# Attention in front of two expert layers: scores in two head orientations, heads alternating in the products with V

## The chip, the cores and the metric

The kernel runs on one core of a Trainium2 chip. The metric is the device time of one execution in microseconds (us). Five engines work side by side and wait for one another through semaphores: PE (TensorE, the matrix multiplier, an array of 128 rows by 128 columns), DVE (VectorE), ACT (ScalarE), POOL (GpSimd) and SP (SyncE, which issues most DMA transfers here). PE reads its operands from on-chip memory and writes into PSUM, which has 8 banks; DVE and ACT read PSUM, POOL can't.

## The reference

Causal attention over 4 sequences of 576 positions with 8 heads of 64, then two layers on the 2304 tokens. Cut to what matters:

```
scores = q @ k.T / 8                                  # per batch and head
cum    = cumsum(max(s, 0))
scores = where(causal, -1e9, scores + min(-(cum_i - cum_j), 0))
attn   = softmax(scores)                              # sum + 1e-9
x      = (attn @ v), heads side by side               # 2304 x 512
h      = x @ w_in;  g = elu(h);  x = g @ w_out        # first layer, 512 -> 2048 -> 512
P      = exp(x @ w_gate), 8 rounds of row and column normalisation
out    = sum over 8 experts of P[:, e] * (relu(x @ w1[e]) @ w2[e])
```

## The kernel before, in words

**Attention.** A job is one pair of heads of one batch: 20 jobs in five chunks. Batch 0 is split in chunk A (queries 0 to 255, 4 jobs) and chunk B (queries 256 to 575, 4 jobs); batches 1 to 3 are F chunks (all queries, 4 jobs each). A job's queries go in items of 64 (an index m from 0 to 8); item m looks at 64(m+1) keys, because of the causal mask. In an item the two heads lie on the two halves of the 128 partitions. There are 144 items.

What an item goes through, with its lines:

- `r_step` (lines 235 to 249): POOL writes a tile R with the bias from cumulated s (line 244, over the item's keys) and adds the causal mask to the last 64 keys (line 247). The tile is one of NR = 6 buffers. The rows of cum that it reads come by DMA (line 222), two per job.
- `qk_piece` (lines 251 to 293): PE forms the scores S, one product per head (line 262): 64 rows by 64 columns of the array each, head 0 in the upper left quarter, head 1 in the lower right one. They are of type fp32, and the trace shows each such product as two matmul instructions. The item of 576 keys takes two PSUM tiles of 288. The pool `ps_s` has two PSUM banks. Then DVE adds S to R and finds the extreme (line 268), ACT takes the exponential with its sum (line 276), DVE the reciprocal (lines 280 and 281), and POOL normalises (line 284).
- `t_piece` (lines 301 to 344): PE transposes R in blocks of 128 keys (line 307). An item with an odd number of 64-key blocks has half a block left, for which 64 columns of the array are used (line 313). ACT copies whole blocks into the tiles aA and aB (lines 319 to 326), DVE the half ones (line 337).
- `pv_piece` (lines 351 to 382): the products X with V, in two halves of the queries (`half` 0: 256 queries, lines 365 and 366; `half` 1: 320 queries, lines 369 to 371). Each uses 128 rows by 64 columns of the array, head 0 in the left columns and head 1 in the right; the last block of line 371 has 64 rows. A call does one head, and a half is two calls one after the other, which the order of the work may separate. The result goes to the x of the first layer through ACT and DVE (`split`, lines 375 to 379).

**Order.** `pieces` (lines 386 to 400) lists score items, transposes four items later (LAG = 4), and products with V. The first layer is a list of groups of 12 matmuls (lines 592 and 624, type fp32r, 128 by 128, with n = 256, 288 or 320 columns). In the main loop the pieces of a chunk are spread over the groups ahead of the first group that needs the chunk (lines 1116 to 1152); `_Flow` is a planner with assumed costs and due times, and it decides when the steps after a matmul are put in the program. The framework that turns the program into queues may then issue work that is ready ahead of work that isn't. The first layer's weights are unpacked by DVE and ACT (`w_decode`, lines 519 to 558) as their turn comes.

**The rest.** After the last attention chunk come the remaining groups of the first layer, a gate, and the second layer (experts), which is matmuls of lines 938 and 1007.

Of the kernel before, what the change touches and what calls it, by code (L numbers as in the profile page):

```python
# [92 lines left out]
def kernel(  # L93
# [16 lines left out]
    NR, LAG, NQK, NCB, NSCAN, NA_T, NH = 6, 4, 2, 2, 1, 1, 5  # L110
# [45 lines left out]

    chunks = CHUNKS
# [3 lines left out]
    spans = {"A": range(0, HALF_A // 64), "B": range(HALF_A // 64, S // 64), "F": range(S // 64)}  # L161
# [3 lines left out]
    for j, (k, b, p, part) in enumerate(jobs):  # L165
# [3 lines left out]
    LAST = S // 64 - 1  # L169
# [3 lines left out]
    cum_m = cst.tile([P, S // 64, B * NPAIR], F32, tag="cum_m", name="cum_m")  # L173
# [7 lines left out]
            att.tile([64, 2, 64], F32, tag=f"a4{i}", name=f"a4{i}"),  # L181
# [29 lines left out]
    def cum_advance():  # L211
        while state["cum"] < NJ:
# [5 lines left out]
            t = att.tile([P, S], F32, tag="cum", name=f"cum{j}", bufs=NCB)  # L218
# [15 lines left out]

    def r_step(i):

        if i >= NI:
            return
        j, m = items[i]
        k, b, p, part = jobs[j]  # L240
        t = att.tile([P, S], F32, tag="R", name=f"R{i}", bufs=NR)
        Rt[i] = t
        n = 64 * (m + 1)
        nc.gpsimd.tensor_scalar(out=t[:, 0:n], in0=ct[j][:, 0:n], scalar1=8.0,  # L244
                                scalar2=cum_m[:, m, b * NPAIR + p : b * NPAIR + p + 1],
# [5 lines left out]
    def qk_piece(i):  # L251
        j, m = items[i]
        sm = att.tile([P, 8], F32, tag="sm", name=f"sm{i}", bufs=6)
        keys = 64 * (m + 1)
        parts = [(0, 288), (288, 288)] if m == LAST else [(0, keys)]
        pss = []
        for c0, n in parts:
            ps = ps_s.tile([P, 512], F32, tag="S", name=f"S{i}_{c0}")
            pss.append(ps)
            for z in range(2):  # L260
                r = slice(64 * z, 64 * z + 64)
                nc.tensor.matmul(ps[r, 0:n], QK[j][r, 0, 64 * m : 64 * m + 64], QK[j][r, 1, c0 : c0 + n],  # L262
                                 start=True, stop=True)
        R = Rt[i]

        def ttr():
            for z, (c0, n) in enumerate(parts):
# [3 lines left out]
            if len(parts) == 2:  # L271
                nc.vector.tensor_tensor(out=sm[:, 2:3], in0=sm[:, 0:1], in1=sm[:, 1:2], op=ALU.min)
# [22 lines left out]
    def qk_cost(i):  # L295
        return 4 * 64 * (items[i][1] + 1) / 2400.0
# [912 lines left out]
```

## Time and profile before

| what | value |
|---|---|
| median of 3 runs | 2264.2 us (2262.67 to 2267.24) |
| the profiled execution | 2263.91 us |
| its span in the trace | 2262.1 us |
| mean granted clock of TensorE | 0.992 of full speed |
| instructions in the trace | 33423 |
| PE busy | 2228.7 us, 99% of the span |
| DVE, ACT, POOL busy | 57%, 42%, 36% of the span |

The profiled execution lies 0.3 us below the median, and 1.8 us of it are outside the span. Times in the trace are counted from the start of the span. A busy PE isn't PE at its full rate: consecutive matmuls overlap, so what an operation costs is read from start to start.

### The profile page before, as it was taken

The numbers are of one execution on the slowest core, as the hardware profiler recorded it, in microseconds if no ns is written. First come the engines' busy times: TensorE is split into PE (matmuls) and PEld (weight loads), VectorE is DVE, ScalarE is ACT, GpSimd is POOL, SyncE is SP. The second block draws the span as 40 slices with busy tenths as digits, with TensorE's granted clock in tenths as the row PEclk, the third lists the DMA queues.
The fourth block names the chain that finished last, engine by engine and source line by source line (L and its number), as shares of the span: only waits on it lengthen the run. The fifth ranks groups of instructions, "written<-read, shape, count | busy, mean of one in ns | idle before, by whom it ended". The sixth has DMA issues, their size and how long they took to land.

```text
span 2262.1 us, 33423 instructions
## 1 busy us (share of the span) xinstructions
PE 2228.7 (99%) x12236; PEld 1920.5 (85%) x12236; DVE 1292.5 (57%) x2891; ACT 943.0 (42%) x2133; POOL 815.9 (36%) x1045
## 2 busy tenths in 40 slices
PE   7999999999999999999999999999999999999999
PEld 3467888887889888888989988889898888998988
DVE  7677687434665765555555455555555555555554
ACT  5554444333442454334343443443443533434332
POOL 7664222232320433343333333333333333333330
PEclk9999999999999899999999999999999999999999
DMA  6443344133274432122223322212214212121121
GB/s 224 137 153 117 125 163 144 54 98 109 85 252 146 139 111 66 56 75 68 72 68 135 120 75 65 75 56 66 75 66 168 98 57 75 66 75 66 58 73 38
DMA packets 99668, 224.36 MB, mean 99 GB/s; under 512 B 8304, under 2 KB 24176, under 8 KB 99504
## 3 DMA queue, kind: packets, MB, share of 16 engines
q1 hardware_dynamic: 94896, 205.45, 27.7%
q10 hardware_dynamic: 4608, 16.78, 1.9%
q8 instruction: 96, 1.57, 0.3%
q14 instruction: 68, 0.56, 0.1%
HBM read 184.90 MB, written 37.30 MB: 98 GB/s over the span
## 4 chain that ended last, share of the span: by engine, by line
PE 94%; DVE 3%; POOL 1%; DMA 1%; issue 1%; ACT 0%; SPq 0%; POOLq 0%; DVEq 0%; ACTq 0%
PE b L1007 35%; PE A L938 17%; PE C L938 9%; PE m L592 9%; PE n L624 8%; PE B L938 4%; PE S L262 4%; PE X L369 3%; PE T L307 2%; PE gate L704 1%; PE X L365 1%; PE X L370 0%; DMA xc_d<-xs 0%; DMA xr<-x_d 0%; PE X L371 0%
## 5 line engine op out<-in xcount | busy, mean ns | idle before, releaser
L1007 PE MATMUL b<-w,h 128*128 128x512 f32 x3456 | 846.1, 393 | 0.0
L1007 PEld LDWEIGHTS b<-w,h 128*128 128x128 f32 x3456 | 645.3, 188 | 125.9
L821 POOL TENSOR_TENSOR w1c<-S,w1c 128x512 fp32r<-128x512 f32 x192 | 264.3, 1400 | 871.1 <-ACT w1c L820 871.1
L938 PE MATMUL A<-xc,w1c 128*128 128x384 f32 x2304 | 449.3, 335 | 0.0
L1021 DVE SCALAR_TENSOR_TENSOR acc<-b,P_t,acc 128x512 f32<-128x512 f32 x264 | 197.4, 748 | 424.8 <-PE b L1007 424.8
L938 PEld LDWEIGHTS A<-xc,w1c 128*128 128x128 f32 x2304 | 405.9, 188 | 8.5
L951 ACT ACTIVATE h<-pre_P 128x384 fp32r<-128x384 f32 x288 | 151.3, 525 | 437.1 <-DVE pre_P L964 437.1
L592 PEld LDWEIGHTS m<-xT,w 128*128 128x128 f32 x1536 | 213.9, 193 | 27.3 <-issue 9.4
L592 PE MATMUL m<-xT,w 128*128 128x288 f32 (+2 forms) x1536 | 234.4, 306 | 2.2 <-DVE r L604 1.1
L938 PE MATMUL C<-xc,w1c 128*128 128x384 f32 x1152 | 233.4, 336 | 0.0
L624 PE MATMUL n<-h,w 128*128 128x288 f32 (+2 forms) x1536 | 226.9, 300 | 3.1 <-DVE r L604 1.6
L624 PEld LDWEIGHTS n<-h,w 128*128 128x128 f32 x1536 | 207.4, 188 | 25.9 <-issue 16.6
L938 PEld LDWEIGHTS C<-xc,w1c 128*128 128x128 f32 x1152 | 205.3, 189 | 8.1
L821 DVE TENSOR_TENSOR w<-sw,w 128x512 fp32r<-128x512 f32 x192 | 154.1, 824 | 61.5 <-ACT w L820 61.5
L244 POOL TENSOR_SCALAR R<-cum,cum_m 128x64 f32<-128x64 f32 (+8 forms) x144 | 91.5, 635 | 223.0 <-PE T L313 176.3
L954 DVE SCALAR_TENSOR_TENSOR h<-pre_P,h 128x384 fp32r<-128x384 f32 x288 | 160.9, 559 | 12.2 <-ACT h L951 0.5
L284 POOL TENSOR_SCALAR R<-R,sm 128x64 f32<-128x64 f32 (+8 forms) x144 | 95.9, 668 | 103.0 <-DVE sm L281 78.5
L951 ACT ACTIVATE h<-A 128x384 fp32r<-128x384 f32 x96 | 47.2, 492 | 193.7 <-PE A L938 193.7
L262 PE MATMUL S<-QK 64*64 64x288 f32 (+8 forms) x640 | 119.3, 440 | 8.6 <-DMA QK<-in_qk_dram 4.6
L820 ACT CAST w<-sw 128x512 fp32r<-128x512 f32 x192 | 109.4, 618 | 22.1 <-DMA w<-w_sc 8.7
L972 ACT COPY pre_P<-A 128x384 f32<-128x384 f32 x192 | 92.3, 481 | 60.5 <-PE A L938 60.5
L938 PE MATMUL B<-xc,w1c 128*128 128x384 f32 x576 | 116.4, 336 | 0.0
(163 smaller groups left out, 2367.4 us busy)
## 6 DMA issues: line engine op xcount, KB each, us to landing
sw<-in_w_dram SPq DMA_DIRECT2D x192, 512.0 KB, 3.3
w<-w_sc SPq DMA_DIRECT2D x56, 512.0 KB, 3.5
w_sc<-w ACTq DMA_DIRECT2D x32, 512.0 KB, 3.0
xc_d<-xs SPq DMA_DIRECT2D x28, 384.0 KB, 3.7
xc<-xc_d SPq DMA_DIRECT2D x14, 768.0 KB, 6.4
QK<-in_qk_dram SPq DMA_DIRECT2D x16, 576.0 KB, 4.6
st<-in_wi_dram SPq DMA_DIRECT2D x16, 512.0 KB, 3.7
st<-in_wo_dram SPq DMA_DIRECT2D x16, 512.0 KB, 4.1
```

The costliest lines, as they stand in the source:

```text
L262: nc.tensor.matmul(ps[r, 0:n], QK[j][r, 0, 64 * m : 64 * m + 64], QK[j][r, 1, c0 : c0 + n], start=True, stop=True)
L284: nc.gpsimd.tensor_scalar(out=R[:, 0:keys], in0=R[:, 0:keys], scalar1=sm[:, 5:6], scalar2=1.0, op0=ALU.mult, op1=ALU.mult)
L592: nc.tensor.matmul(ps[:, 0:n], t[:, a, d * P : (d + 1) * P], x[:, z, d, c0 : c0 + n], start=(d == 0 and o == 0), stop=(d == 3 and o == 2))
L624: nc.tensor.matmul(ps[:, 0:n], t[:, a, f * P : (f + 1) * P], h[:, z, c0 : c0 + n], start=(f == 0 and o == 0), stop=(f == 3 and o == 2))
L820: nc.scalar.copy(hi, x)
L821: eng.tensor_tensor(out=lo, in0=x, in1=f32(hi), op=ALU.subtract)
L938: nc.tensor.matmul(ps, t[:, a, wi_, kt * P : (kt + 1) * P], x[:, z, kt], start=(first and kt == 0 and o == 0), stop=(kt == 1 and o == 2), ...
L951: nc.scalar.activation(h[:, 0], src, AF.Relu)
L954: nc.vector.scalar_tensor_tensor(out=h[:, 1], in0=src, scalar=0.0, in1=f32(h)[:, 0], op0=ALU.max, op1=ALU.subtract)
L972: nc.scalar.copy(new(name), ps)
L1007: nc.tensor.matmul(ps, h[:, z, c0 : c0 + P], t[:, a, :], start=(f == 0 and o == 0), stop=(f == 3 and o == 2))
L1021: nc.vector.scalar_tensor_tensor(out=a, in0=ps, scalar=q, in1=a, op0=ALU.mult, op1=ALU.add)
```

## The change

Items are gathered in sets whose scores are issued together. In the B and F chunks the items 0, 1, 3, 6 and 7 have the two heads swapped on the partitions (`swapped`): head 0's scores go to partitions 64 to 127 and head 1's to 0 to 63, which are the two quarters of the array that the other items don't use. A set has a PSUM bank for each orientation. An F job has three sets, a B job three, an A job two (no item swapped). The rows of cum and the per-item scalars exist in both orders, so a B or F job loads two more rows of cum. The bias tiles of items 0 to 4 of an F job share one large buffer (`Rs`, one buffer), NR goes from 6 to 5 with 640 columns, and the bias is written over whole 128-key blocks. The last block of a transpose is 128 wide. Where an item is swapped, its copies after the transpose are made per head. The products with V alternate the heads at each step, in one call, all in the shape 128 by 64 (`a4` has 128 partitions, of which the lower half is zero). Transposes come one set later (two sets in chunk A) instead of four items later, and a product with V that is due is put right in front of the next set's scores.

```diff
-    NR, LAG, NQK, NCB, NSCAN, NA_T, NH = 6, 4, 2, 2, 1, 1, 5
+    NR, NQK, NCB, NSCAN, NA_T, NH = 5, 2, 2, 1, 1, 5
...
+    TAIL = 512
+    SWAP = (0, 1, 3, 6, 7)
+
+    SETS = {"A": [[0, 1], [2, 3]], "B": [[4], [5, 7, (LAST, TAIL)], [LAST, 6]],
+            "F": [[0, 1, 2, 3, 4], [5, 7, (LAST, TAIL)], [LAST, 6]]}
...
-            for z in range(2):
-                src = s if j < NSCAN else cum_d
-                nc.sync.dma_start(t[64 * z : 64 * z + 64, 0:keys],
-                                  src[row + z : row + z + 1, 0:keys].partition_broadcast(64))
+            for w in range(1 if part == "A" else 2):
+                n = TAIL if w else keys
+                for z in range(2):
+                    h = row + (z ^ w)
+                    nc.sync.dma_start(t[64 * z : 64 * z + 64, w, 0:n],
+                                      src[h : h + 1, 0:n].partition_broadcast(64))
...
-        nc.gpsimd.tensor_scalar(out=t[:, 0:n], in0=ct[j][:, 0:n], scalar1=8.0,
+        w = (n + 127) // 128 * 128
+        z = swapped(i)
+        nc.gpsimd.tensor_scalar(out=t[:, 0:w], in0=ct[j].rearrange("p w k -> p (w k)")[:, S * z : S * z + w], scalar1=8.0,
...
+    def qk_set(n):
+        banks, streams, cols = {}, {}, {}
+        for i, c0, keys in sets[n]:
+            z = swapped(i)
+            if z not in banks or cols[z] + keys > 512:
+                banks[z] = ps_s.tile([P, 512], F32, tag="S", name=f"S{i}_{c0}")
+                cols[z] = 0
...
+        while any(streams.values()):
+            z = min((z for z in streams if streams[z]), key=lambda z: done[z])
...
+            for h in range(2):
+                r = slice(64 * h, 64 * h + 64)
+                o = slice(64 * (h ^ z), 64 * (h ^ z) + 64)
+                nc.tensor.matmul(ps[o, at : at + keys], QK[j][r, 0, 64 * m : 64 * m + 64],
+                                 QK[j][r, 1, c0 : c0 + keys], start=True, stop=True)
...
+        def by_head(x, out, eng):
+            if z:
+                for h in range(2):
+                    eng(out[:, h], x[:, 1 - h])
+            else:
+                eng(out, x)
...
-            for c in range(3):
-                nc.tensor.matmul(x[r, 0:320], vj[:, h, c], aB[:, h, c, :], start=(c == 0), stop=False)
-            nc.tensor.matmul(x[r, 128:320], vj[:, h, 3], aB[:, h, 3, 128:320], start=False, stop=False)
-            nc.tensor.matmul(x[r, 256:320], vj[0:64, h, 4], a4[:, h, :], start=False, stop=True)
...
+            steps = [(c, aB[:, :, c, :], 0, 320) for c in range(3)]
+            steps += [(3, aB[:, :, 3, 128:320], 128, 320), (4, a4, 256, 320)]
+        for n_, (c, a, x0, x1) in enumerate(steps):
+            for h in range(2):
+                nc.tensor.matmul(x[64 * h : 64 * h + 64, x0:x1], vj[:, h, c], a[:, h], start=(n_ == 0),
+                                 stop=(n_ == len(steps) - 1))
...
-    for i in range(NI + LAG + 2):
-        if i < NI:
-            pieces.append((jobs[items[i][0]][0], qk_cost(i), "qk", i))
+    for n in range(len(sets) + 4):
+        due = []
+        while pend and pend[0][0] <= n:
+            _, j, half = pend.pop(0)
+            due.append((jobs[j][0], pv_cost(j, half), "pv", (j, half)))
+        if n < len(sets):
+            due.append((set_chunk[n], set_cost(n), "qk", n))
+        if due:
+            bundles.append(due)
+        while emitted < len(sets) and emitted + (2 if set_chunk[emitted] == 0 else 1) <= n:
```

## Rows read from the trace of the kernel before

**Rows 1.** The page, parts 1 and 4: engines, and the chain that ended last.
```profile
PE 2228.7 (99%) x12236; PEld 1920.5 (85%) x12236; DVE 1292.5 (57%) x2891; ACT 943.0 (42%) x2133; POOL 815.9 (36%) x1045
...
PE 94%; DVE 3%; POOL 1%; DMA 1%; issue 1%; ACT 0%; SPq 0%; POOLq 0%; DVEq 0%; ACTq 0%
```

**Rows 2.** Windows: length, PE, PEld, DVE, ACT, POOL busy, granted clock, DMA share, GB/s.
```profile
0.00:39.00 39.00, 25.63 (x122) 13.03 (x122) 26.98 (x104) 17.05 (x56) 25.51 (x61) 0.96 0.64 213
39.00:107.00 68.00, 65.10 (x360) 34.17 (x359) 47.36 (x181) 37.98 (x102) 46.52 (x78) 1.00 0.50 166
107.00:205.00 98.00, 98.00 (x590) 61.12 (x590) 75.55 (x277) 54.86 (x156) 66.38 (x108) 1.00 0.44 147
205.00:425.00 220.00, 220.00 (x1503) 182.68 (x1502) 153.29 (x461) 94.73 (x246) 61.21 (x108) 1.00 0.36 123
425.00:590.00 165.00, 164.98 (x1110) 133.30 (x1109) 79.80 (x283) 64.25 (x175) 48.83 (x95) 0.97 0.30 94
```

**Rows 3.** Timeline of PE, 299 to 309 us: start, length, instruction, count.
```profile
299.62 0.65 PE L262 MATMUL S<-QK 64*64 64x256 f32 x4
300.20 1.70 PE L592 MATMUL m<-xT,w 128*128 128x256 f32 x12
...
303.80 0.76 PE L262 MATMUL S<-QK 64*64 64x320 f32 x4
304.49 2.02 PE L592 MATMUL m<-xT,w 128*128 128x320 f32 x12
306.44 1.83 PE L369 MATMUL X<-aB,V 128*64 128x320 f32 x6
...
308.78 4.58 PE L624 MATMUL n<-h,w 128*128 128x256 f32 x36
```

**Rows 4.** Timeline of PE, 317 to 342 us.
```profile
317.17 3.68 PE L592 MATMUL m<-xT,w 128*128 128x320 f32 x24
320.69 0.27 PE L313 MATMUL T<-ident,R 128*64 128x128 f32 x1
...
327.93 0.27 PE L307 MATMUL T<-ident,R 128*128 128x128 f32 x1
328.04 0.27 PE L313 MATMUL T<-ident,R 128*64 128x128 f32 x1
328.07 2.01 PE L624 MATMUL n<-h,w 128*128 128x320 f32 x12
330.00 1.08 PE L262 MATMUL S<-QK 64*64 64x512 f32 x4
331.01 3.79 PE L624 MATMUL n<-h,w 128*128 128x320 f32 x24
...
341.19 0.65 PE L365 MATMUL X<-aA,V 128*64 128x256 f32 x2
...
341.99 1.85 PE L592 MATMUL m<-xT,w 128*128 128x288 f32 x12
```

**Rows 5.** Timeline of PE, 39 to 41 us: head 0's L366 beside head 1's L365.
```profile
39.97 0.32 PE L366 MATMUL X<-aA,V 128*64 128x128 f32 x1
39.98 0.43 PE L365 MATMUL X<-aA,V 128*64 128x256 f32 x1
40.13 0.27 PE L366 MATMUL X<-aA,V 128*64 128x128 f32 x1
40.25 0.38 PE L365 MATMUL X<-aA,V 128*64 128x256 f32 x1
```

**Rows 6.** Groups by line and shape: operation, count, busy us, mean ns, idle before.
```profile
L268 DVE CUSTOM_DVE_ANT_0 R<-S,R 128x512 f32<-128x512 f32 x16 | 11.0, 689 | 3.7 <-PE S L262 1.9 <-POOL R L247 1.5
...
L326 ACT COPY aB<-T 128x256 f32<-128x256 f32 x16 | 5.9, 370 | 12.7 <-PE T L313 12.5
```

**Rows 7.** DMA issues: transfers of cum, count, KB each, us to landing.
```profile
cum<-cum_d SPq DMA_DIRECT2D x32, 144.0 KB, 3.2
```

**Rows 8.** Waits of PE's weight loads: engine, line waited for, us, times, longest.
```profile
PEld T L307 <- POOL R L284: 12.3, 11, 2.5
```

More of the change, by code (lines that the diff above doesn't have):

```diff
@@ L252, in qk_piece, with softmax @@
+    def softmax(i, c0, n, ps, base):
         j, m = items[i]
-        sm = att.tile([P, 8], F32, tag="sm", name=f"sm{i}", bufs=6)
         keys = 64 * (m + 1)
[L255 to L263, printed above, removed]
@@ L285, in norm, with set_cost @@
                                     op0=ALU.mult, op1=ALU.mult)
-        c = qk_cost(i)
         d = keys / 950.0
-        flow.after(c + 0.05, ttr)
-        flow.after(c + 0.25 + d, ex)
-        flow.after(c + 0.6 + 2 * d, rec)
-        flow.after(c + 0.8 + 2 * d, norm)
-        return c + 1.2 + 3.2 * d
-    def qk_cost(i):
-        return 4 * 64 * (items[i][1] + 1) / 2400.0
+        flow.after(base, ttr)
+        if last:
+            flow.after(base + 0.2 + d, ex)
+            flow.after(base + 0.55 + 2 * d, rec)
+            flow.after(base + 0.75 + 2 * d, norm)
+            ready["t", i] = flow.now + base + 1.15 + 3.2 * d
+        return base + 0.1 + n / 950.0
+    def set_cost(n):
+        t = [0, 0]
+        for i, c0, keys in sets[n]:
+            t[swapped(i)] += keys
+        return 4 * max(t) / 2400.0
     def t_cost(i):
-        return (items[i][1] // 2 + 1) * 0.06
+        return (items[i][1] // 2 + 1) * 0.11
     def t_piece(i):
@@ L383, in pv_piece @@
             flow.after(pv_cost(j, half) + 0.1, lambda: v_load(j + 2))
-    pieces = []
+    sets, set_r, set_t = [], [], []
+    set_chunk = []
+    for j, (k, b, p, part) in enumerate(jobs):
+        at = {m: job_items[j][0] + x for x, m in enumerate(spans[part])}
+        seen_r = set()
+        for x in SETS[part]:
+            parts = [(m, 0) if isinstance(m, int) else m for m in x]
+            sets.append([(at[m], c0, 64 * (m + 1) - c0 if c0 else min(TAIL, 64 * (m + 1))) for m, c0 in parts])
+            set_r.append([at[m] for m, _ in parts if m not in seen_r])
+            seen_r |= {m for m, _ in parts}
+            set_t.append([at[m] for m, c0 in parts if not c0])
+            set_chunk.append(k)
@@ L401 @@
[L401 to L402 removed]
+            due.append((jobs[j][0], pv_cost(j, half), "pv", (j, half)))
[4 more added lines that the diff above has]
+        while emitted < len(sets) and emitted + (2 if set_chunk[emitted] == 0 else 1) <= n:
+            for t in set_t[emitted]:
+                j, m = items[t]
+                for x in [x for x in pend if x[1] != j and x[2] == (m > 3)]:
+                    pend.remove(x)
+                    bundles.append([(jobs[x[1]][0], pv_cost(*x[1:]), "pv", x[1:])])
+                bundles.append([(jobs[j][0], t_cost(t), "t", t)])
+                if m == 3 or t == job_items[j][1] - 1:
+                    pend.append((n + 1, j, 0 if m == 3 else 1))
+            emitted += 1
@@ L403 @@
+    assert not pend
+    chunk_cost = [sum(c for x in bundles for kk, c, _, _ in x if kk == k) for k in range(NCHUNK)]
+    chunk_last = [max(i for i, x in enumerate(bundles) if any(y[0] == k for y in x)) for k in range(NCHUNK)]
     ready = {}
```

180 lines of the change are left out of this document (102 added, 78 removed).

## The prediction

> **What bounds the kernel now.** I read the page first: PE is busy in 99% of the span and holds 94% of the chain that ended last [rows 1]. So a microsecond of PE time that goes is a microsecond of span, as long as nothing else takes over. Then I cut the attention's part of the span into stages with the view by windows [rows 2]. Up to 39 us PE is busy in 25.6 of 39 us: chunk A waits for its own chain. From 39 to 107 us (mostly chunk B) and from 107 to 205 us (the first F chunk) PE is full, but DVE is at 70% and 77% and POOL at 68% in both. From 205 to 425 us and from 425 to 590 us, with four F jobs each, PE is full, DVE at 70% and 48%, POOL under 30%. The reader is to see that PE binds everywhere after 39 us, with little room behind it before 205 us and much after. Behind 590 us there is no attention, and nothing there changes.
>
> Last I read the timeline of PE from start to start, where it never idles [rows 3, 4].
>
> **Scores.** 256 keys take 0.58 us (299.62 to 300.20) and 512 keys 1.01 us (330.00 to 331.01) [rows 3, 4]: 1.68 ns a key and 0.15 us besides. The neighbours pay too: two groups of 12 matmuls of 320 columns take 3.52 us undisturbed (317.17 to 320.69), 1.76 each [rows 4], but the one between scores and X takes 1.95 (304.49 to 306.44) [rows 3]. That is 0.19 more, so a visit of PE to a small shape costs 0.34 us beside its columns. An F job before: 2880 keys, 4.84 us, and nine visits, 3.06, together 7.90. After, if the two orientations overlap: three sets, each as long as its longer stream of 512 keys, 0.86 + 0.34 = 1.20, together 3.60. It saves 4.3 us a job. If they don't overlap, only six visits go, 2.0 us a job; that is the other bound. I take the first: in the rows the two heads of one item already share the array, since a key takes four matmul columns (two heads, two instructions each), and at the pace of X below, 0.3 us for 320 columns, these would take 3.8 ns one after the other and not 1.68.
>
> **Products with V.** One head of half 1 takes 2.34 us (306.44 to 308.78) and, with 0.19 at the neighbours, 2.53; one head of half 0 0.80 (341.19 to 341.99) and 0.99 [rows 3, 4]. Its six matmuls of 320 columns fill 1.83 us of that [rows 3], 0.3 each: they go one after the other. Alternating, both heads should take what one takes: 3.5 us less per F job. The bound below is no gain. I take the gain because the trace holds one place where the queue had head 0's L366 and head 1's L365 side by side: they start 0.01 us apart, at 39.97 and 39.98, and L365's second matmul follows 0.27 us after its first although L366 runs beside it [rows 5]. Both use all 128 rows, each its own 64 columns.
>
> The Trainium skill (TensorE: Matmul & The Clock Gate, section The mechanism) says that weight loads overlap running matmuls only where the row group differs, and that matmuls start and end strictly in program order. By that, alternating heads on the same rows would gain nothing here and the sum would be some 36 us smaller; the starts above speak against it.
>
> **Transposes.** A whole block takes 0.11 us (327.93 to 328.04). A half one takes 0.03 and makes the next group longer: 1.93 against 1.76 (328.07 to 330.00), of which the score visit behind it has about half [rows 4]. So a half block costs 0.03 to 0.20, likeliest 0.11; over 80 of them the change gains or loses up to 7 us. I take nothing.
>
> **Other engines.** Split copies: five more on ACT and two more on DVE per F job, each at most the 0.37 us of a copy of 256 columns, the nearest row [rows 6]: below 2 us on ACT and 0.8 on DVE. POOL writes 320 more columns of 2880 per F job in one of its three steps, below 11% of its time; both hide behind PE after 205 us and add to the load before. Two more loads of cum for each of 16 jobs land in 3.2 us [rows 7] and are issued a job ahead; uncovered, the first B job would pay that once. SP issues them between weights, none of which PE waited for long. What is late next is DVE: a set needs all its additions of S before the next set gets its two banks, up to 0.69 us each [rows 6].
>
> **The sum, by stage.** An F job loses 4.3 + 3.5 = 7.8 us of PE. A B job: five visits and 2240 keys, 5.46, become three sets (320, 512, 512 keys), 3.28; with 2.5 from X it loses 4.7. An A job loses two visits and 0.99, 1.7.
> - 0 to 39 us: PE isn't the bound; between 0 and 7, I take 2.
> - 39 to 107 us: PE would shrink by 19, to 49, with DVE's 47.4 and POOL's 46.5 inside it. No row shows DVE over 77%; at that it needs 61.5 us, a saving of 6. Between 6 and 19, I take 9.
> - 107 to 205 us: PE falls by 31 to 67, below DVE's 75.6. At 77% DVE saves nothing, at 100% 22. I take 13, which is 85 us with DVE at 89%: its rows here are many small steps of separate items, so some of its idle time can be filled.
> - 205 to 590 us: 62, with DVE at 81% of the first 189 us; I take 60.
>
> Together 84 us. The profiled execution took 2263.9 us, 0.3 below the median, and becomes 2180 us.
>
> **The rivals.**
> 1. PE stays the bound throughout and the early stages keep their PE savings: 7 + 19 + 31 + 62 = 119 us, 2145 us. For it: POOL and DVE aren't full now. Against it: both would have to be at 95% or more.
> 2. DVE takes over. It has the additions of S, the copies, the unpacking of weights and the first layer's results, and none of that shrinks. Held at 77%, the stages give 2, 6, 0, 21 and 31 us, 60 in all, 2204 us. For it: [rows 2]. Against it: 77% is what DVE was asked for, not what it can do. The Trainium skill (TensorEngine Tiling (Array Packing), section PSUM Bottleneck) warns that tiling speeds up the array and not the emptying of PSUM, which may then be the bottleneck.
> 3. The two orientations don't overlap, because they read the same rows of the array, or because the framework issues them apart: 2.3 us less in each of eight jobs and some 5 in the early stages, 2203 us.
> 4. The heads of X don't overlap, as when each load of weights waits for the other head's matmul: 3.5 us in eight jobs and 8 earlier, 2216 us. [Rows 5] speak against it.
> 5. Slower: PE stands in front of transposes that aren't ready. PE takes its queue in order, and a set's transposes now follow one set later, with up to five items' chains (addition, exponential, reciprocal, normalisation) behind one another and one shared bias buffer. Before, PE's weight loads waited for POOL's normalisation 11 times, 12.3 us in all, 2.5 at most [rows 8]. There are 56 sets; from 1.5 us of waiting per set the gain is gone, and at 2.5 us it costs 140: 2320 us. Against it: after 107 us first-layer groups lie between the sets, and the planner and the framework put them where the chain isn't done.
>
> About 0.2% (4.5 us) is what can be told from no change.
>
> **How the numbers follow.** The forecast has 0.57, rival 1 0.13, rival 2 0.13, rivals 3 and 4 0.05 each, rival 5 0.04. The remaining 0.03 is for waits that just eat the gain, within 0.2%. So faster 0.93, same 0.03, slower 0.04. The range goes from rival 1, 2145, to a little past rivals 2 and 3, 2210; rivals 4 and 5 and the tie stay outside.
>
> **What would show it.** A set of 512 keys a stream should take about 1.0 us from start to start, both heads of half 1 about 2.3, of half 0 about 0.8, and a transposed block still 0.11. The stages up to the last attention matmul (590 us before) should end near 506 us, with DVE over 80% between the first F job and the second F chunk. If sets take 1.7 us or more, step "scores" is wrong; if half 1 takes over 4 us, step "V". If PE is idle before transposes by tens of microseconds, rival 5 holds; if attention ends near 470 us, rival 1.

## The result, and the profile after

The kernel after takes 2212.0 us (median of 4 runs, 2207.6 to 2214.5) against 2264.9 for the kernel before beside it: a ratio of 0.9764, 95% interval 0.9745 to 0.9783. It is 53 us faster, where 84 were forecast, and lies 2 us above the range. The profiled execution took 2213.0 us, with a span of 2211.2.

Lines have moved: scores are L302 (L262 before), additions of S L321 (L268), biases and masks L273 and L276 (L244, L247), normalisation L337 (L284), transposes L364, and L367 and L370 for last blocks (L307, L313), products with V L431 (L365 to L371), groups of the first layer L677 and L709 (L592, L624).

The page of the kernel after, engines and chain, against [rows 1]:

```profile
PE 2151.1 (97%) x12236; PEld 1901.1 (86%) x12236; DVE 1294.1 (59%) x2921; ACT 940.2 (43%) x2201; POOL 823.3 (37%) x1046
...
PE 88%; DVE 5%; POOL 2%; DMA 1%; ACT 1%; issue 1%; SPq 0%; POOLq 0%; DVEq 0%; ACTq 0%
```

PE's busy time fell by 77.6 us, and the span by 50.9 alone. (The prediction's savings of PE add up to 119 us, in its rival 1; part of what PE still does runs at a lower clock, as shown below.) PE, which stood idle for 33 us of the span before, now stands for 60, and DVE and POOL hold 7% of the chain instead of 4%. The windows of the kernel after (columns as in [rows 2]) say where:

```profile
0.00:39.00 39.00, 22.41 (x108) 11.73 (x108) 21.66 (x84) 13.29 (x42) 23.32 (x59) 0.88 0.56 177
39.00:107.00 68.00, 56.16 (x297) 28.77 (x296) 42.87 (x161) 33.21 (x97) 42.22 (x70) 0.82 0.50 171
107.00:205.00 98.00, 85.27 (x622) 58.22 (x623) 80.10 (x306) 60.90 (x194) 72.46 (x118) 0.95 0.54 178
205.00:425.00 220.00, 217.48 (x1707) 198.74 (x1707) 175.19 (x543) 105.62 (x308) 81.50 (x132) 0.99 0.40 139
425.00:590.00 165.00, 161.76 (x1261) 148.48 (x1260) 97.44 (x302) 72.59 (x208) 56.08 (x90) 0.97 0.37 122
```

From 39 to 107 us PE was full before, and every engine is idler now: PE 56 of 68 us, DVE 43, POOL 42. The granted clock of the window is 0.82. No engine is the bound there; they wait for one another. From 205 us PE is at 98% to 99%, nearly as full as it was.

A table by stages shows it best. An end is the start of the last matmul of a chunk's products with V, in one profiled execution; times of one kernel differ by up to 7 us here (2207.6 to 2214.5), so a few us between the ends of two runs tell nothing by themselves.

| end of | before | after | after, against the forecast |
|---|---|---|---|
| chunk A | 48.8 | 58.0 | 9.2 later; forecast 2 sooner (to 39 us) |
| chunk B | 106.8 | 122.4 | 15.6 later; forecast 11 sooner |
| first F chunk (F1) | 203.9 | 209.7 | 5.8 later; forecast 24 sooner |
| second (F2) | 418.5 | 389.2 | took 179.4, not 214.6 |
| third (F3) | 598.6 | 545.5 | took 156.4, not 180.1 |
| first layer | 736.6 | 685.6 | 140 behind F3's end, 138 before |

F2 and F3 give 58.9 us, where 60 were forecast from 205 us on. Up to F1's end 30 us are missing: 24 forecast, 5.8 lost. That is the whole miss, but for 1 us in F2 and F3 and 2 us behind them.

What the rows forecast of PE's operations came about. The timeline of PE of the kernel after in F2, which answers to [rows 3, 4]:

```profile
296.15 2.16 PE L431 MATMUL X<-aB,V 128*64 128x320 f32 x16
298.14 0.28 PE L431 MATMUL X<-a,V 128*64 128x64 f32 x4
298.35 1.09 PE L302 MATMUL S<-QK 64*64 64x384 f32 x12
299.37 3.46 PE L677 MATMUL m<-xT,w 128*128 128x256 f32 x24
```

Both heads of half 1 take 2.20 us (296.15 to 298.35), where one took 2.34. The set of items 5, 7 and the last 64 keys of 8 (448 keys in one orientation, 512 in the other) takes 1.02 us (298.35 to 299.37). Now the end of chunk A and chunk B in the same view, with the idle time before a row and what ended it in brackets, and two windows of the same stretch:

```profile
56.96 0.44 PE L364 MATMUL T<-ident,R 128*128 128x128 f32 x2 [1.71 <-POOL R L337]
...
62.62 0.66 PE L364 MATMUL T<-ident,R 128*128 128x128 f32 x4 [1.85 <-POOL R L337]
...
68.12 1.11 PE L364 MATMUL T<-ident,R 128*128 128x128 f32 x4 [2.48 <-POOL R L337]
...
76.33 4.11 PE L431 MATMUL X<-aB,V 128*64 128x320 f32 x16
80.22 0.41 PE L431 MATMUL X<-a,V 128*64 128x64 f32 x4
...
82.20 0.93 PE L364 MATMUL T<-ident,R 128*128 128x128 f32 x7
83.06 1.08 PE L302 MATMUL S<-QK 64*64 64x512 f32 x4
...
89.11 2.16 PE L431 MATMUL X<-aB,V 128*64 128x320 f32 x16
91.10 0.28 PE L431 MATMUL X<-a,V 128*64 128x64 f32 x4
```

```profile
64.00:80.00 16.00, 12.72 (x49) 4.79 (x43) 7.24 (x32) 6.98 (x19) 8.30 (x13) 0.50 0.38 136
81.00:92.00 11.00, 9.76 (x66) 5.25 (x66) 8.45 (x33) 8.04 (x24) 7.96 (x13) 1.00 0.30 97
```

At 76 us the two heads take 4.2 us, at 89 us 2.2: the windows give a granted clock of 0.50 (1.2 GHz) from 64 to 80 us and 1.00 (2.4 GHz) from 81 us. The lower clock begins at 63.4 us. Ahead of it PE had stood for 1.71 and 1.85 us before transposes, and it does again, for 2.48, at the lower clock, each time for POOL's normalisation. Between the first full clock and 140 us the granted clock is the lower one for 41.0 us, against 3.4 before.

What those transposes wait for: the waits of PE's weight loads over the whole span, against [rows 8], and POOL's timeline ahead of one such wait, with the reciprocal on DVE that the normalisation needs and the transposes on PE:

```profile
PEld T L364 <- POOL R L337: 27.8, 18, 3.4
```

```profile
97.51 0.15 DVE L334 RECIPROCAL sm<-sm 128x1 f32<-128x1 f32 x1
...
99.60 1.16 POOL L273 TENSOR_SCALAR R<-cum,cum_m 128x512 f32<-128x512 f32 x2
100.84 0.32 POOL L276 TENSOR_TENSOR R<-R,mask 128x64 f32<-128x64 f32 x1
101.26 0.38 POOL L273 TENSOR_SCALAR R<-cum,cum_m 128x128 f32<-128x128 f32 x1
101.72 0.32 POOL L276 TENSOR_TENSOR R<-R,mask 128x64 f32<-128x64 f32 x1
102.12 0.48 POOL L273 TENSOR_SCALAR R<-cum,cum_m 128x256 f32<-128x256 f32 x1
102.68 0.60 POOL L276 TENSOR_TENSOR R<-R,mask 128x64 f32<-128x64 f32 x2
103.26 0.53 POOL L337 TENSOR_SCALAR R<-R,sm 128x320 f32<-128x320 f32 x1
...
103.85 0.44 PE L364 MATMUL T<-ident,R 128*128 128x128 f32 x2 [0.98 <-POOL R L337]
```

The 0.5 us normalisation has its reciprocal at 97.7 us and runs at 103.3: it stands behind the biases and masks of the next set, which POOL takes in the order of its queue. PE stands idle for the 0.98 us up to 103.85, since what is behind the transposes doesn't pass them.

### The profile page after: what moved, and what is told of

The parts are those of the page before. It is cut to its first block, busy times and chain, and to the rows that moved or that the text cites. A ratio compares the mean times of both kernels' runs of the same rounds, so it can differ in the third digit from the quotient of the medians.

```text
span 2211.2 us, 33504 instructions
## 1 busy us (share of the span) xinstructions
PE 2151.1 (97%) x12236; PEld 1901.1 (86%) x12236; DVE 1294.1 (59%) x2921; ACT 940.2 (43%) x2201; POOL 823.3 (37%) x1046
## 4 chain that ended last, share of the span: by engine, by line
PE 88%; DVE 5%; POOL 2%; DMA 1%; ACT 1%; issue 1%; SPq 0%; POOLq 0%; DVEq 0%; ACTq 0%
PE b L1092 36%; PE A L1023 18%; PE C L1023 9%; PE n L709 7%; PE m L677 7%; PE B L1023 5%; PE S L302 2%; PE X L431 2%; PE T L364 1%; PE gate L789 1%; DVE R L321 1%; POOL R L273 1%; DVE h L692 0%; DMA xr<-x_d 0%; DVE r L689 0%
## 5 line engine op out<-in xcount | busy, mean ns | idle before, releaser
L677 PE MATMUL m<-xT,w 128*128 128x288 f32 (+2 forms) x1536 | 231.3, 305 | 2.9 <-DVE r L689 1.5
L709 PE MATMUL n<-h,w 128*128 128x288 f32 (+2 forms) x1536 | 222.3, 299 | 3.3 <-DVE r L689 1.6
L677 PEld LDWEIGHTS m<-xT,w 128*128 128x128 f32 x1536 | 214.2, 194 | 12.4 <-issue 5.0
L709 PEld LDWEIGHTS n<-h,w 128*128 128x128 f32 x1536 | 207.3, 188 | 17.3 <-issue 11.1
L1039 DVE SCALAR_TENSOR_TENSOR h<-pre_P,h 128x384 fp32r<-128x384 f32 x288 | 160.8, 558 | 12.3 <-ACT h L1036 0.5
L273 POOL TENSOR_SCALAR R<-cum,cum_m 128x256 f32<-128x256 f32 (+4 forms) x144 | 101.8, 707 | 155.5 <-PE T L370 90.6
L337 POOL TENSOR_SCALAR R<-R,sm 128x64 f32<-128x64 f32 (+8 forms) x144 | 92.5, 650 | 118.6 <-DVE sm L334 64.0
L1023 PEld LDWEIGHTS B<-xc,w1c 128*128 128x128 f32 x576 | 104.6, 190 | 7.8 <-issue 0.2
```

Source lines behind the costliest of these rows:

```text
L273: nc.gpsimd.tensor_scalar(out=t[:, 0:w], in0=ct[j].rearrange("p w k -> p (w k)")[:, S * z : S * z + w], scalar1=8.0, scalar2=cum_m[:, z, m ...
L337: nc.gpsimd.tensor_scalar(out=R[:, 0:keys], in0=R[:, 0:keys], scalar1=sm[:, 5:6], scalar2=1.0, op0=ALU.mult, op1=ALU.mult)
L677: nc.tensor.matmul(ps[:, 0:n], t[:, a, d * P : (d + 1) * P], x[:, z, d, c0 : c0 + n], start=(d == 0 and o == 0), stop=(d == 3 and o == 2))
L709: nc.tensor.matmul(ps[:, 0:n], t[:, a, f * P : (f + 1) * P], h[:, z, c0 : c0 + n], start=(f == 0 and o == 0), stop=(f == 3 and o == 2))
L1023: nc.tensor.matmul(ps, t[:, a, wi_, kt * P : (kt + 1) * P], x[:, z, kt], start=(first and kt == 0 and o == 0), stop=(kt == 1 and o == 2), ...
L1039: nc.vector.scalar_tensor_tensor(out=h[:, 1], in0=src, scalar=0.0, in1=f32(h)[:, 0], op0=ALU.max, op1=ALU.subtract)
```

## The experiments

Theory: PE's savings are real, and the early stages lose them because PE's queue waits for the softmax chain (DVE, ACT, POOL), which the sets bring closer. Rivals: one engine is simply full (POOL, or DVE with the unpacking of weights), or the lower clock is the cause. Each ratio below is against the kernel before on the same chip, with its 95% interval; that of the kernel after is 0.9764 [0.9745, 0.9783].

### Are the savings real?

**heads_in_turn**: the heads one after the other in the call of X.

```diff
-        for n_, (c, a, x0, x1) in enumerate(steps):
-            for h in range(2):
+        for h in range(2):
+            for n_, (c, a, x0, x1) in enumerate(steps):
```

> The changed kernel, but in the products with V all steps of head 0 come first and then all of head 1, in one call. It prices the alternation. By the reading that alternating heads run side by side, the products of half 1 go from 2.2 us to about 4.3 us and those of half 0 from 0.8 us to about 1.5 us, 2.8 us per F job, 22 us in the two later F chunks and some in the earlier ones: 2232 to 2247 us. If alternation is worth nothing, 2212 us within 5 us.

2232.4 us, 0.9845 [0.9825, 0.9865]. The time is as expected, its parts aren't: F2 and F3 take 183.1 and 163.0 us, 10.3 more than after and not 22. Its timeline of PE:

```profile
304.00 2.15 PE L431 MATMUL X<-aB,V 128*64 128x320 f32 x9
305.99 0.22 PE L431 MATMUL X<-a,V 128*64 128x64 f32 x1
306.00 0.43 PE L431 MATMUL X<-aB,V 128*64 128x320 f32 x1
306.05 0.22 PE L431 MATMUL X<-a,V 128*64 128x64 f32 x1
306.26 1.56 PE L431 MATMUL X<-aB,V 128*64 128x320 f32 x6
...
307.87 1.09 PE L302 MATMUL S<-QK 64*64 64x384 f32 x12
...
327.63 0.88 PE L431 MATMUL X<-aA,V 128*64 128x256 f32 x8
328.44 1.07 PE L302 MATMUL S<-QK 64*64 64x512 f32 x8
```

Half 1 takes 3.87 us, 1.67 more than alternating. But the edit doesn't put the heads in turn everywhere on PE. In half 1 head 1's first matmul (320 columns) starts at 305.68, ahead of head 0's last ones (64 columns, 305.99 and 306.05), so the two overlap there. In half 0 the single matmuls of the trace still start in pairs 0.01 us apart (327.63 and 327.64, 327.89 and 327.91), and both heads take 0.81 us, one head's time in [rows 4]. Why PE's order differs from the program's there is not shown. So the run prices alternation in half 1 alone: what is in turn costs more, what still starts in pairs doesn't.

**no_swap**: no item is swapped, so a set has one orientation.

```diff
-    SWAP = (0, 1, 3, 6, 7)
+    SWAP = ()
```

> The changed kernel without swapped items: the same sets, but all items in the first orientation, so that each F set has 960 keys in one stream, over two banks. It prices the four quarters. By the reading that two orientations run side by side, an F set goes from about 1.02 us to about 1.8 us, 2.3 us more per F job and less for ACT and DVE (fewer split copies); 18 us in the two later F chunks, so 2225 to 2235 us. If the four quarters don't matter for the time because something else binds, 2212 us within 5 us.

2239.1 us, 0.9882 [0.9866, 0.9899], a little past what was expected. The set of item 8's first 512 keys and item 6's 448 now takes 1.75 us (338.91 to 340.66), where in the kernel after, in two orientations, it takes 1.01 (320.27 to 321.28; its rows come first):

```profile
320.27 1.08 PE L302 MATMUL S<-QK 64*64 64x512 f32 x8
321.28 7.31 PE L709 MATMUL n<-h,w 128*128 128x320 f32 x48
```

```profile
338.91 1.83 PE L302 MATMUL S<-QK 64*64 64x512 f32 x8
340.66 3.79 PE L709 MATMUL n<-h,w 128*128 128x320 f32 x24
```

F2 and F3 take 190.2 and 163.1, 17.4 us more in eight jobs or 2.2 each. The prediction's rival 3 had priced a lost overlap at 2.3.

**before_heads_alternate**: the kernel before with one thing of the change alone, both heads of X in one call and alternating (with `a4` of 128 partitions).

```diff
-            for h in range(2):
-                pieces.append((jobs[j][0], pv_cost(j, half) / 2, "pv", (j, h, half)))
+            pieces.append((jobs[j][0], pv_cost(j, half), "pv", (j, half)))
```

> The kernel before with one part of the change alone: the two heads alternate in the products with V, in one call, all in the 128 by 64 shape. By the sum, 3.5 us less for each of the eight later F jobs, 28 us, and up to 24 us from the earlier jobs as far as PE binds there, of which I expect 5 to 10: 2226 to 2234 us. If the two heads don't run side by side, 2262 to 2268 us.

2221.6 us, 0.9811 [0.9791, 0.9831]: better than expected. F2 and F3 take 197.9 and 168.1 us, 28.7 less than before; the step "products with V" says 8 x 3.5 = 28. The rest of the change takes another 30.2 off them in the kernel after; the step "scores" says 34. And F1 ends at 186.4 us, 17.4 sooner than before and 23.3 sooner than after. So the early stages could use PE's savings, and it is the rest of the change (sets, order, buffers) that costs them. All of the 23.3 us is there by chunk B's end (98.8 us here, 122.4 after); F1 itself takes 87.6 us here and 87.4 after. In its windows PE is full again:

```profile
39.00:107.00 68.00, 65.51 (x394) 33.76 (x394) 53.58 (x206) 42.14 (x115) 51.76 (x89) 0.96 0.56 179
107.00:205.00 98.00, 97.63 (x675) 69.13 (x674) 80.59 (x286) 57.83 (x161) 66.62 (x106) 1.00 0.46 155
```

DVE and POOL do more here per microsecond than in the kernel after (53.6 and 51.8 us of 68, against 42.9 and 42.2). Neither was full there.

### Which wait?

**warm_clock**: three extra products of 128 x 128 x 128, whose result nobody reads, ahead of each item's transposes in chunks A and B.

```diff
+            for _ in range(3):
+                nc.tensor.matmul(dummy[:, 0:P], ident, ones, start=True, stop=True)
```

> The changed kernel with three more products (128 by 128 by 128, fp32, result unused) in front of the transposes of each item of chunks A and B, 36 items. At full clock they are some 0.64 us an item, 23 us in all, that PE has to do where it does not stand idle. Theory CLOCK: the work keeps the clock up, the lower clock's 41 us before 140 us shrink below 20, chunk B ends earlier than 122 us and the time is below 2207 us. If the low clock is a consequence of the waits and costs little by itself, chunk B ends 5 to 20 us later than 122 us and the time is 2217 to 2232 us.

2211.2 us, 0.9757 [0.9742, 0.9772]: no change, and neither theory's numbers. The lower clock falls from 41.0 to 20.5 us and the first B job ends at 68.7 us instead of 80.3, though PE does more; chunk B's end comes 7 us sooner (115.0), F1's 5 (204.8). With half of the lower clock gone the time stays. The edit adds some 23 us of work to PE, so what the lower clock costs by itself stays open; that it follows from the waiting is suggested by its beginning behind the waits, and not shown by an edit.

**lag2_chunk_b**: transposes two sets later in chunk B too.

```diff
-        while emitted < len(sets) and emitted + (2 if set_chunk[emitted] == 0 else 1) <= n:
+        while emitted < len(sets) and emitted + (2 if set_chunk[emitted] <= 1 else 1) <= n:
```

> The changed kernel, but in chunk B the transposes come two sets after their scores, as in chunk A, and not one. Two theories of why the attention up to the end of chunk B got 15 us longer (107 to 122 us) instead of shorter. Theory ORDER: PE takes its queue in order and stands in front of transposes of the set just issued, whose chain of addition, exponential, reciprocal and normalisation isn't done; then chunk B ends 8 us or more earlier (by 114 us) and the time falls to 2204 us or below. Theory BUFFERS: five bias buffers hold back POOL's next bias, and a longer hold makes it worse; then chunk B ends at 122 us or later and the time is 2212 us or above.

2202.9 us, 0.9715 [0.9693, 0.9737]. The time is as expected, chunk B's end (118.8, 3.6 sooner) isn't; F1 ends at 201.3.

**early_as_before**: chunks A and B item by item, unswapped, transposes four items later, with five buffers.

```diff
-    SETS = {"A": [[0, 1], [2, 3]], "B": [[4], [5, 7, (LAST, TAIL)], [LAST, 6]],
+    SETS = {"A": [[0], [1], [2], [3]], "B": [[4], [5], [6], [7], [(LAST, TAIL), LAST]],
```

> The changed kernel, but chunks A and B go item by item as in the kernel before: no swapped items, each item a set of its own, transposes four items later; the F chunks stay in sets. Heads still alternate in the products with V everywhere, transposes are full-width, five bias buffers. Theory ORDER (the sets of chunks A and B make PE wait): chunk B ends by 107 us or earlier and the time is 2186 to 2197 us. Theory BUFFERS or extra work (more loads of cum, wider bias, five buffers): those stay, chunk B still ends near 122 us and the time stays within 5 us of 2212 us.

2208.9 us, 0.9747 [0.9733, 0.9762]: not what was expected. The first two B jobs end at 65.9 and 78.3 us, as in the kernel before (64.2, 78.4), the last two at 98.9 and 116.4 (91.6, 106.8). The loss of chunk A is undone, and a loss comes back in the second half of chunk B. F1's first set with its five biases is one candidate. Another is that this version writes the bias and mask of item 8 twice in each B job (148 biases in its trace, 144 in the kernel after), as told below; neither was tried on this version.

**norm_on_act**: up to F1, ACT normalises instead of POOL.

```diff
+            if jobs[j][0] <= 2:
+                nc.scalar.activation(R[:, 0:keys], R[:, 0:keys], AF.Copy, scale=sm[:, 5:6])
+                return
```

> The changed kernel, but in chunks A and B and in the first F chunk ACT normalises in place of POOL. Theory POOL QUEUE: POOL works in order, a set's biases are issued all at once, and from 93.9 to 103.3 us eleven biases and masks stand in front of the normalisation that PE's transposes wait for; without the normalisations in that queue chunk B ends by 110 us instead of 122 and the time falls to 2200 us or below. Theory CLOCK (PE is slow up to 140 us because it runs at the lower clock for 41 us of it) and theory ORDER (a set's transposes come too soon after its scores) both expect no gain from this alone: chunk B within 4 us of 122, time 2207 to 2217 us.

2200.2 us, 0.9712 [0.9697, 0.9728]. Chunk B ends at 106.3 us, 16 sooner, as theory POOL QUEUE says. PE's loads for transposes, which waited 27.8 us for POOL's normalisation, wait 2.6 us in 3 waits for ACT's. F1 then takes 97 us instead of 87 and ends at 203.5, so 10 of the 16 us are lost again there; why isn't settled. POOL has 28.2 of 68 us left to do, and still PE isn't full:

```profile
39.00:107.00 68.00, 58.42 (x350) 31.20 (x350) 41.44 (x176) 48.48 (x131) 28.15 (x55) 0.89 0.51 166
```

**late_bias**: a set's biases are put into POOL's queue just ahead of its scores, not one set ahead, up to F1.

> The changed kernel, but up to the first F chunk the biases of a set are issued just before its scores and not with the scores of the set before, so that POOL has the normalisations of the set before the last ahead of them. Theory POOL QUEUE: transposes wait less, chunk B ends 5 us or more earlier (by 117 us), 2207 us or below. Against it: a set's additions of S then wait for its biases, up to 4.5 us for five of them; if that wait is longer than the one removed, chunk B ends later than 122 us and the time is 2215 us or above.

2208.0 us, 0.9747 [0.973, 0.9763]; B ends at 115.5, F1 at 202.4. Both are sooner, but the time's interval overlaps that of the kernel after. **lag2_norm_on_act**, both edits named, doesn't add:

> The version whose chunk B has its transposes two sets later (2202.9 us), and ACT normalises up to the first F chunk. If POOL QUEUE and ORDER are two causes that add, it lies below both single edits, at 2185 to 2195 us, with chunk B ending by 107 us. If they are one and the same wait, it lies within 4 us of the better of the two.

2208.3 us, 0.9748 [0.9734, 0.9763], slower than norm_on_act alone; the interval overlaps that of lag2_chunk_b.

**less_unpacking**: for the first 16 weights three of DVE's operations in their unpacking are left out, and with them the low part of these weights; this takes work off DVE alone.

> The changed kernel, but the first 16 weights of the first layer are unpacked without three of DVE's seven steps (the low part of the weights is left out), 1.9 us of DVE for each weight, 30 us over the first 210 us. Theory DVE: in the first F chunk DVE is the bound (92% to 100% from 160 to 180 us), so its end, at 209.7 us in the changed kernel, comes 10 us or more earlier than the end of chunk B explains, and the time is 2203 us or below. Theory POOL QUEUE alone: the end of chunk B stays near 122 us and the first F chunk still takes 87 us; 2208 to 2216 us.

2192.6 us, 0.9686 [0.967, 0.9701]: 19 us, the most of any single edit; B ends at 101.4, F1 at 190.8. F1 itself takes 89 us, 2 more than after, which speaks against DVE as the bound of F1: theory DVE has the time right and the place wrong. DVE's work ahead of chunk B's end counts as POOL's does. These weights are also ready sooner for the first layer, and the run doesn't tell the two apart. The kernel after has DVE at 96% from 160 to 180 us, yet at 63% from 39 to 107, where this edit gains most (the first row is of the kernel after, the second of this one):

```profile
160.00:180.00 20.00, 17.33 (x145) 13.24 (x144) 19.20 (x71) 14.35 (x45) 14.15 (x22) 1.00 0.65 214
```

```profile
39.00:107.00 68.00, 59.55 (x385) 31.04 (x381) 46.88 (x192) 41.03 (x123) 48.25 (x84) 0.97 0.72 240
```

**norm_on_act_less_unpacking**, the same part left out, again doesn't add:

> ACT normalises up to the first F chunk, and the first 16 weights are unpacked without three of DVE's seven steps, so the low part of these weights is left out. With POOL's queue relieved chunk B ended at 106 us and the first F chunk at 203.5 us, 97 us after it, with DVE at 90% to 100% from 150 to 190 us. Theory DVE: the first F chunk now takes 85 us or less and the time falls to 2190 us or below. If DVE isn't the bound, the first F chunk still takes 95 us or more and the time stays within 4 us of 2200 us.

2195.2 us, 0.9692 [0.9672, 0.9713]; F1 takes 98.6 us behind chunk B's end (104.2), which again speaks against DVE as its bound. **norm_on_act_add_on_pool** moves one addition of the unpacking of the first 16 weights from DVE to POOL, which has room once ACT normalises:

> ACT normalises up to the first F chunk and, complete in its results, POOL makes one of the seven unpacking steps (the addition, 0.73 us on DVE) of the first 16 weights: 12 us less for DVE in the first 210 us, some 6 of them in the first F chunk. Theory DVE: 2193 to 2198 us. If DVE isn't the bound, or if POOL's slower addition delays the weights, 2200 us or above.

2213.0 us, 0.9773 [0.9758, 0.9787], a miss: F1 ends at 210.2. An addition takes POOL 1.32 us up to 205 us, where DVE takes 0.83 in the kernel after. That the slower weights are what PE then waits for is likely and not shown.

### Which part of the change?

Two parts of it were put singly into before_heads_alternate (2221.6 us). **alternate_five_buffers**: NR = 5.

> The kernel before with alternating heads (2221.6 us, first F chunk ends at 186.4 us) and five bias buffers in place of six. Theory BUFFERS: POOL's next bias waits for a transposed tile, the first F chunk ends at 195 us or later and the time is 2230 us or above. If the buffers aren't the cause, it ends by 190 us and the time stays within 4 us of 2221.6 us.

2226.7 us, 0.9832 [0.9817, 0.9846], between the two expectations; F1 ends 6.5 us later. The intervals overlap, so 5 us is a likely size and no more. **alternate_lag_two**: transposes two items later instead of four.

> The kernel before with alternating heads (2221.6 us) and transposes two items after their scores in place of four, which is about what a lag of one set amounts to. Theory ORDER: PE stands in front of transposes whose chain isn't done, the first F chunk ends at 196 us or later and the time is 2231 us or above. If the distance isn't the cause, within 4 us of 2221.6 us.

2231.7 us, 0.9855 [0.9833, 0.9877]: 10 us. The waits of PE's weight loads up to 205 us show it (9.7 us in 9 waits in before_heads_alternate):

```profile
PEld T L307 <- POOL R L284: 19.8, 17, 7.0
```

But chunk A has already lost 7.5 us at its end (59.2 against 51.7), and there the kernel after keeps a lag of two sets, four items. From there to F1's end this run is only 1.9 us slower. It shows what a short lag costs where the chain has no cover, not that it explains chunk B.

The other way round, **items_then_sets** takes the kernel after and goes item by item through A, B and F1, with six buffers and a lag of four; F2 and F3 keep their sets. **items_then_sets_from_first_f** does so in A and B alone.

> Chunks A, B and the first F chunk item by item as before (no swapped items, transposes four items later, six buffers of 576 columns), the two later F chunks in sets as in the changed kernel; heads alternate everywhere. If the sets are what costs in the stages with little other work for PE, the first F chunk ends near 186 us, the rest takes the changed kernel's 2002 us, and the time is 2184 to 2194 us, faster than both kernels. If the early loss has another cause (extra loads, wider bias, full-width transposes), 2200 us or above.

> As the version with items up to the first F chunk, but that chunk in sets: only chunks A and B go item by item, with six buffers. It prices the sets of the first F chunk alone, among them five biases at once in POOL's queue while chunk B runs. Theory ORDER with POOL's queue: chunk B ends 8 us or more later than with items in the first F chunk and the time is 10 to 20 us above that version. If sets are harmless in the first F chunk, within 4 us of it, or below it by the 10 us and more that PE saves.

2203.5 us for both, 0.9725 [0.971, 0.9739] and 0.9723 [0.9707, 0.9739]; F1 ends at 198.4 and 203.6, chunk B at 105.2 and 113.6. The second has chunk B's end as expected, 8.4 us later with F1 in sets, but not the time. The first is a miss: the items and the lag of before_heads_alternate, and F1 ends 12 us later. POOL has more to do from 39 to 205 us. Its biases there in before_heads_alternate and in items_then_sets, of all widths and then those of 576 columns alone:

```profile
L244 POOL TENSOR_SCALAR R<-cum,cum_m 128x384 f32<-128x384 f32 (+8 forms) x64 | 44.5, 695 | 28.2 <-PE T L313 14.6 <-PE T L307 8.4 <-PE T53b L313 1.1
...
L244 POOL TENSOR_SCALAR R<-cum,cum_m 128x576 f32<-128x576 f32 x9 | 8.0, 884 | 1.9 <-PE T L313 1.1
```

```profile
L276 POOL TENSOR_SCALAR R<-cum,cum_m 128x512 f32<-128x512 f32 (+4 forms) x75 | 54.8, 731 | 19.5 <-PE T L367 7.5 <-PE T L373 5.9
...
L276 POOL TENSOR_SCALAR R<-cum,cum_m 128x576 f32<-128x576 f32 x17 | 13.7, 808 | 3.4 <-PE T L373 1.9
```

Wider columns can make no more than the difference of the means, 36 ns each or 2.7 us. The rest is the count, 11 more biases, and 8 of these are of 576 columns. A set that names item 8 twice, `[(LAST, TAIL), LAST]`, has its bias and mask written twice, into two of the six buffers. items_then_sets and the two runs below do so in the eight jobs of B and F1 (152 biases in their traces, not 144), early_as_before and items_then_sets_from_first_f in the four of B. With a mean of 0.81 us for such a bias and 0.39 for a mask, that is some 9.6 us of POOL from 39 to 205 us that before_heads_alternate doesn't have. No run goes item by item from the kernel after without it, so these runs don't price single items cleanly, and this rival for the 12 us stands untested. **items_then_sets_narrow** cuts the biases back to the item's own keys, and the last transpose to 64 columns:

```diff
-        w = min((n + 127) // 128 * 128, S)
+        w = min((n + 127) // 128 * 128, S) if k > 2 else n
```

> The kernel that went item by item up to the end of the first F chunk and in sets behind it (2203.5 us), with the biases and the last half block's transpose of those first three chunks cut back to the item's own keys and to 64 columns, as in the kernel before. Theory POOL'S COLUMNS (POOL was busy 130 us between 39 and 205 us there, against 118 us in the kernel before with heads alternating alone, and that is what its first F chunk ended 12 us later for): the last product with V of the first F chunk falls from 198 us to 188 to 192, and the time to 2192 to 2198. Rival ORDER IN THE BUNDLE (the products with V and the scores stand in another order on PE there): 196 us or later, and 2201 to 2206.

2207.9 us, 0.9752 [0.9736, 0.9769]; F1 ends at 204.1, later. The width of POOL's biases isn't it; the second bias of item 8 is still there. **items_then_sets_narrow_free** also puts products with V and scores into the order singly (and cuts the last item at 288 keys, as before), where the kernel after makes them one bundle, with the scores behind the products:

```diff
-        if n < len(sets):
+        if n < len(sets) and set_chunk[n] <= 2:
+            bundles.append([(set_chunk[n], set_cost(n), "qk", n)])
+            bundles += [[d] for d in due]
+            due = []
+        elif n < len(sets):
             due.append((set_chunk[n], set_cost(n), "qk", n))
```

> The same, and in those three chunks the products with V no longer bundled with the scores of an item (each is put in the order by itself, as in the kernel before), so that up to the end of the first F chunk it has the structure of the kernel before with heads alternating alone, and behind it that of the kernel after. Theory (PE's order and the pieces on POOL cause the loss of the early stages, and the gains of the two later F chunks are independent of it): the first F chunk ends at 186 to 190 us, the second and third take 177 to 182 and 155 to 160 us, and the time is 2186 to 2194, below every kernel so far that computes the whole. Rival (the two are not independent; what is saved early is waited for later): first F chunk 186 to 190, but the time 2198 or more.

2196.3 us, 0.9702 [0.9688, 0.9717]: 11.6 us below the run before it, with F1's end at 192.3 and F2 and F3 at 179.0 and 157.8. The end of F1 and the time miss their ranges by 2 us each, but the early gain does add to those of F2 and F3, within a few us. The edit changes three things at once: the bundles, the order of scores and products with V, and the last item's cut. From 107 to 205 us (narrow, then free), PE's and DVE's busy times rise together:

```profile
107.00:205.00 98.00, 90.12 (x599) 58.96 (x599) 77.11 (x272) 54.77 (x156) 74.67 (x123) 0.95 0.45 157
```

```profile
107.00:205.00 98.00, 92.75 (x670) 67.17 (x670) 84.25 (x297) 58.31 (x170) 74.39 (x121) 0.98 0.50 164
```

By the program, a bundle is put in when the latest of its parts is due, so the scores wait for the copies that the products with V need, and the next chain starts that much later. That this is where the 11.6 us come from is argued and not shown. This kernel is faster than both kernels compared here (its interval ends at 0.9717, that of the kernel after begins at 0.9745). Of those that compute the whole it has the lowest median; norm_on_act's interval overlaps with it, and the two together weren't tried.

## Why the prediction was wrong, point by point

**Scores: right.** A set of 512 keys was put at about 1.0 us and takes 1.02; in F2 and F3 the kernel after saves 30.2 of the 34 us.

**Products with V: right.** Both heads of half 1 were put at about 2.3 us and take 2.20; the run with this part alone gives 28.7 where 28 were forecast. The rule on weight loads in the Trainium skill (TensorE: Matmul & The Clock Gate, section The mechanism), that they overlap running matmuls only where the row group differs, would leave no gain there; the trace disagrees, 2.20 us for both heads against 2.34 for one. The same page's table of measured packings (section Measured speedup vs the span model) does list a gain for tiles in different columns, and the trace agrees with that.

**Transposes: right.** Seven blocks take 0.86 us (82.20 to 83.06), 0.12 each, where 0.11 was forecast.

**Other engines: right where PE covers them.** From 205 to 425 us DVE is at 80% and F2 gives its 35 us. The warning in the Trainium skill (TensorEngine Tiling (Array Packing), section PSUM Bottleneck) that tiling speeds up the array and not the emptying of PSUM fits one listed wait here, and a small one: up to 205 us PE's loads for scores waited 6.6 us in 7 waits for DVE's additions of S.

**The sum, by stage: wrong in its first three terms** (2, 9 and 13 us; measured, to the nearest ends of chunks, 9.2 lost, 6.4 lost, 9.7 won). This is the step that failed. The terms from 39 us on let each stage shrink until its fullest engine came to a share of 80 to 89%, as if DVE and POOL could be kept that full, and put the waiting of PE's queue at nothing. In the kernel after nothing is that full from 39 to 107 us: POOL is at 62%, DVE at 63%, and PE's loads for transposes wait 27.8 us for POOL's normalisation up to 205 us. With that link taken off POOL chunk B ends 16 us sooner and the kernel is 12 us faster (norm_on_act). So what counts there is the chain from scores to products with V against the work that PE has meanwhile. The change lengthens the first by putting a set's biases together into POOL's queue (up to three in chunk B, five in F1) and shortens the second; that bundling the scores lengthens it too is likely. [Rows 2] had the warning: up to 39 us PE was busy in 25.6 of 39 us with no engine full, a stage that goes by its chain. The last term, 60 us, came out as 58.9.

**Rival 5 was the right mechanism in the wrong size.** PE does stand before transposes that aren't ready, 27.8 us in 18 waits instead of 12.3 in 11. What stood against it, first-layer groups between the sets after 107 us, holds after 205 us alone: all 18 waits lie before, and 11 of them, 15.6 us, from 107 to 205 us. In chunk B there are few such groups; none starts from 63.7 to 81.9 us. Its point of decision, 1.5 us per set over 56 sets, was set against the whole gain, not against the early stages' own 24 us.

**Rival 2** (2204 us) is near by its total, not by its stages: it has 52 us from 205 us on and 8 before.

**Still open:** of the 23.3 us between F1's ends in the kernel after and in before_heads_alternate, the last edit (bundles, order and cut together) is worth some 12 in one base and five buffers some 5 in another; the rest isn't settled, nor what the second bias of item 8 costs. Small edits move F1's end by about 6 us either way (items_then_sets against narrow); the planner's order and the differences between executions can both do that, so smaller causes can't be told apart. The attention's end before was 598.6 us by the last product with V, not the 590 of the forecast.

## What to carry to other kernels

Shares of busy time tell what an engine could still take only where one engine is full; where an in-order queue waits for a chain through other engines, look for what is issued ahead of the link that ends last, and see that independent work (here the next scores) isn't tied to it. Price a change per stage, and put a packing of the array first where there is cover: here sets for the later chunks and single items for the first ones beat both kernels.

## What the runs showed of the hardware

- Two matmuls of 128 rows by 64 columns each, side by side on the same rows with different weights, run at the pace of one if they start in pairs 0.01 us apart: 2.20 us for 20 of them. Where most of them start one after the other, the 20 take 3.87.
- The four quarters of the array work at once: a set of 512 and 448 keys takes 1.01 us in two orientations, 1.75 in one.
- Two waits of 1.7 and 1.9 us within 6 us, with PE busy between them, came ahead of 17 us at a granted clock of 1.2 GHz, in which the same products took 4.2 us instead of 2.2.
